# Strassen's seven products in the first layers of the last four blocks of an attention and maxout kernel

## The chip, the cores and the metric

The kernel runs on one core of a Trainium2 chip. The metric is the device time of one execution in microseconds (us), lower is better. TensorE multiplies matrices into PSUM, VectorE and ScalarE carry the results from PSUM to SBUF, GpSimd adds in SBUF and issues the input loads, and SyncE (SP) issues the output stores and the transposing DMAs. Each engine works through its own instructions in program order.

## The reference, cut to what matters

```python
# q, k, v: (8, 8, 576, 64); keys and values are averaged over groups of 8 tokens
k_p = k.reshape(B, H, 72, 8, 64).mean(axis=3)
v_p = v.reshape(B, H, 72, 8, 64).mean(axis=3)
attn = softmax(q @ k_p.T / 8)              # 576 x 72 per batch and head
x = (attn @ v_p), heads side by side       # (4608, 512): 8 batches of 576 tokens
h = max(max(x @ w1, x @ w2), x @ w3)       # (4608, 768)
out = h @ w_out                            # (4608, 512), float32
```

## The kernel before

**The maxout layer.** With w1 taken out, h = x w1 + max(0, x (w2 - w1), x (w3 - w1)). The kernel forms w2 - w1 and w3 - w1 once (`sub_w`, kept in `mw1` and `mw2`), and the product w1 w_out once (`linear`, kept in `wm`). So the first layer is two products followed by a maximum with zero, and the second layer adds two products in one PSUM bank: x times `wm` and the maximum times `mwo`.

**Blocks.** The 4608 tokens are cut into nine blocks of 512 (0 to 8). `block(n, plan)` runs `hidden(n)` and then `project(n)`. In `hidden`, each of six column groups `jc` of 128 takes two parts (`hidden_part`): four matmuls of 512 columns per part into a `pw` bank (line 321); after the first part ScalarE takes the relu into `t` (L327), after the second VectorE takes the larger of `t` and the bank into `hT` (L329). `project` makes four tiles of 128 tokens: four matmuls x by `wm` (L353), six matmuls `hT` by `mwo` (L357) into one `po` bank, a ScalarE copy to `osb` (L362), and two stores on SP.

**Attention in between.** Every part and every half of an output tile is a slot, and `plan(n)` hangs attention steps of batch n + 1 on the slots: `k` (transpose the keys into `kz`, L171 and L176), `s0` to `s7` (scores of one head, 576 columns, and their exponential on ScalarE, L199 and L204), `v0` to `v4` (values of 128 tokens, L234, then a reciprocal and a product on VectorE into `xn`, L240 and L242), `x0` to `x4` (bring `xn` into `xT`; from batch 3 on by a transposing DMA on SP, L219), and `T` (transpose the queries of batch n + 2 into `qT` by a DMA on SP, L265). Since a batch has 576 tokens and a block 512, block 5 (tokens 2560 to 3071) reads batch 4 and the slices x0 and x1 of batch 5, written x50 and x51 below. `pool_work(n)`, at the first slot of block n, puts on GpSimd the loads of batch n + 3 (keys, values, queries; the first waits for the first matmuls of the block) and then the sums over groups of 8 for batch n + 2 (`fold_k`, `fold_v`).

**What sets the order.** There is no scheduler: instructions are issued in the order written, and an engine stops at the first instruction whose inputs or buffer are not ready. PSUM's eight banks are shared out as `tr` 1, `pw` 3, `att` 2 x 2. SP's queue holds query transposes, slices and stores in one line.

Of the kernel before, what the change touches and what calls it, by code (L numbers as in the profile page):

```python
# [14 lines left out]
def kernel(  # L15
# [18 lines left out]
    C = H * D  # L34
# [19 lines left out]
    sb3 = ctx.enter_context(tc.tile_pool(name="sb3", bufs=3))  # L54
    psp = ctx.enter_context(tc.tile_pool(name="psp", bufs=1, space=PSUM))
    ctx.enter_context(tc.manual_schedule())

    kts, vts, qbs, kps, qTs, ets = {}, {}, {}, {}, {}, {}
# [90 lines left out]
    def pool_v(b, h, g, tag, evac):  # L149

        pvp = psp.tile([128, g - h, D], F32, name="pvp", tag=tag[0], bufs=tag[1])
        for j in range(POOL):
            nc.tensor.matmul(pvp, identh[0:Sp, :], vts[b][:, h:g, j, :],  # L153
                             start=(j == 0), stop=(j == POOL - 1))
        evac(out=vp_all[:, b, h:g, 0:D], in_=pvp[0:Sp])

    def turn_q(b, n0, n1, evac, tag):
        if b not in qTs:
            qTs[b] = sb2.tile([128, 2 * NG, 128], BF16, name="qT", tag="qT")
        pqt = psp.tile([128, n1 - n0, 128], BF16, name="pqt", tag=tag[0],  # L160
                       bufs=tag[1])
        qf = qbs[b].rearrange("p hp t d -> p (hp t d)")
        for n in range(n0, n1):
            nc.tensor.transpose(pqt[:, n - n0, :], qf[:, 128 * n:128 * n + 128],  # L164
                                ident)
        evac(out=qTs[b][:, n0:n1, :], in_=pqt)

    def keys(b, tag):
        pkt = psp.tile([128, 6, 96], BF16, name="pkt", tag=tag[0], bufs=tag[1])
        for i in range(6):  # L170
            nc.tensor.transpose(pkt[:, i, :], kps[b][:, i, :, :], ident[0:96, 0:96])  # L171
        return pkt
# [7 lines left out]
    def turn_k(b):  # L180
        pkt = keys(b, ("att", 2))
        for par in range(2):
            fill_kz(b, par, 0, H, pkt, nc.vector.tensor_copy)

    def pool_k(b, tag):

        new_kp(b)
        pkp = psp.tile([128, 6, D], F32, name="pkp", tag=tag[0], bufs=tag[1])
        for j in range(POOL):
            nc.tensor.matmul(pkp, identh[0:96, :], kts[b][:, :, j, :],  # L190
                             start=(j == 0), stop=(j == POOL - 1))
        nc.vector.tensor_copy(out=kps[b][:, :, 0, :], in_=pkp[0:96])
        nc.scalar.copy(out=kps[b][:, :, 1, :], in_=pkp[0:96])
# [15 lines left out]
    def scores(b, h):  # L209
        psc = psp.tile([128, 1024], F32, name="psc", tag="att", bufs=2)  # L210
        score(b, h, psc[:, 0:320], 0, 0, 5)
        score(b, h, psc[:, 320:512], 1, 0, 3)
        score(b, h, psc[:, 512:576], 1, 3, 4)
        exp(ets[b][:, h, :], psc[0:Sp, 0:S])

    def turn_x(b, c0, keep, xn, tag, evac=nc.scalar.copy):
        if b > 2:
            g0 = S * b + c0
            nc.sync.dma_start_transpose(  # L219
                out=xT[:, :, g0 + keep:g0 + 128],  # L220
                in_=xn.rearrange("p g h d -> p (g h d)")[keep:128])
            return
        pxt = psp.tile([128, KCH, 128], F16, name="pxt", tag=tag[0], bufs=tag[1])
        for kc in range(KCH):
            nc.tensor.transpose(  # L225
                pxt[:, kc, :],
                xn[:, kc // 2, 2 * (kc % 2):2 * (kc % 2) + 2, :], identh)
        g0 = S * b + c0
        evac(out=xT[:, :, g0 + keep:g0 + 128], in_=pxt[:, :, keep:128])

    def values(b, c0):
        pav = psp.tile([128, 2, 512], F32, name="pav", tag="att", bufs=2)
        for h in range(H):
            nc.tensor.matmul(  # L234
                pav[:, h // 4, 65 * (h % 4):65 * (h % 4) + 65],
                ets[b][:, h, c0:c0 + 128], vp_all[:, b, h, :],
                start=True, stop=True)
        pv = pav[:, :, 0:260].rearrange("p g (h e) -> p g h e", e=65)
        rcp = sb3.tile([128, 2, 4], F32, name="rcp", tag="rcp")
        nc.vector.reciprocal(out=rcp, in_=pv[:, :, :, 64])  # L240
        xn = sb3.tile([128, 2, 4, D], F16, name="xn", tag="xn", bufs=6)
        nc.vector.tensor_tensor(  # L242
            out=xn, in0=pv[:, :, :, 0:D],
            in1=rcp.to_broadcast([128, 2, 4, D]), op=ALU.mult)
        return xn

    CHUNKS = ((0, 0), (128, 0), (256, 0), (384, 0), (448, 64))
    TR = ("tr", 1)
    PW = ("pw", 3)
# [4 lines left out]
    def do(b, steps):  # L254
# [3 lines left out]
        for name in steps.split():  # L258
# [4 lines left out]
            elif name[0] == "T":  # L263
                qTs[b] = sb2.tile([128, 2 * NG, 128], BF16, name="qT", tag="qT")
                nc.sync.dma_start_transpose(  # L265
                    out=qTs[b], in_=qbs[b].rearrange("p hp t d -> p (hp t d)"))
            elif name[0] == "k":
                turn_k(b)
            elif name[0] == "K":
                fold_k(b, nc.vector)  # L270
            elif name[0] == "p":
                pool_v(b, 4 * i, 4 * i + 4, TR, nc.scalar.copy)
            elif name[0] == "s":
                if i == 0:
                    new_et(b)
                scores(b, i)
            elif name[0] == "d":
                sub_w(i)
            elif name[0] == "w":
                turn_w(i, nc.scalar.copy if i % 2 else nc.vector.tensor_copy)  # L280
            elif name[0] == "v":
                xns[b, i] = values(b, CHUNKS[i][0])
            else:
                turn_x(b, *CHUNKS[i], xns[b, i], ("att", 2),
                       nc.vector.tensor_copy if name[0] == "X" else nc.scalar.copy)
# [11 lines left out]
    def turn_w(jc, evac):  # L297
        pwt = psp.tile([128, KCH, 128], F16, name="pwt", tag=TR[0], bufs=TR[1])
        for kc in range(KCH):
# [3 lines left out]
    def linear():  # L303

        for kc in range(KCH):
            pm = psp.tile([128, C], F32, name="pm", tag="pw", bufs=3)
            for jc in range(JCH):
# [8 lines left out]
    def hidden_part(n, jc, c0, c1, hT):  # L316
        col = slice(NB * n + c0, NB * n + c1)
        for wi in range(1, 3):
            pw = psp.tile([128, c1 - c0], F32, name=f"pw{wi}", tag="pw", bufs=3)
            for kc in range(KCH):  # L320
# [11 lines left out]

    def hidden(n, hT):

        halves = n < 2
        if halves:
# [7 lines left out]

    def project(n, hT):
        for mm in range(4):
# [3 lines left out]
            for c in ((slice(0, C // 2), slice(C // 2, C)) if last else (slice(0, C),)):  # L350
                po = psp.tile([128, c.stop - c.start], F32, name="po", tag="pw", bufs=3)
                for kc in range(KCH):
                    nc.tensor.matmul(po, xT[:, kc, bass.ts(m, 128)], wm_sb[:, kc, c],  # L353
                                     start=(kc == 0), stop=False)
                yield
                for jc in range(JCH):
                    nc.tensor.matmul(po, hT[:, jc, bass.ts(mm, 128)], wo_sb[:, jc, c],  # L357
                                     start=False, stop=(jc == JCH - 1))
# [10 lines left out]

    def new_hT():  # L370
        return sb2.tile([128, JCH, NB], F16, name="hT", tag="hT")


    wm = psp.tile([128, 512], F32, name="wm", tag="tr", bufs=1)

# [4 lines left out]
    new_et(0)  # L380
    ATT = ("att", 2)
    new_kp(0)
    k16 = const.tile([96, 6, 4, D], F16, name="k16", tag="k16")
    pkp0 = psp.tile([128, 6, D], F32, name="pkp", tag="pw", bufs=3)
    heat(10)
# [32 lines left out]
    def scores4(h):  # L418
        psc = psp.tile([128, 4, 256], F32, name="psc4", tag="att", bufs=2)
        for i in range(4):  # L420
# [3 lines left out]
    def scores2(h):  # L424
        psc = psp.tile([128, 2, 512], F32, name="psc2", tag="att", bufs=2)
        for i in range(2):
# [26 lines left out]

    def block(n, plan):

        hT = new_hT()
        slot = 0
        for part in (hidden(n, hT), project(n, hT)):
            for _ in part:
                if slot == 0 and n > 0:  # L460
                    pool_work(n, mms[-1])
                for b, steps in plan.get(slot, ()):
                    if b < B:
                        do(b, steps)
                slot += 1

# [6 lines left out]
              29: [(1, "s4 s5")], 30: [(1, "s6 s7")], 31: [(1, "v0")],  # L473
              32: [(1, "v1 x0")], 33: [(1, "X1 v2")]})
    load_k(3, nc.gpsimd)
# [16 lines left out]
    def plan(n):  # L492
# [5 lines left out]
        return got  # L498

    def pool_work(n, mm):  # L500

        if n + 3 < B:
            after([load_k(n + 3, nc.gpsimd)], mm)
            load_v(n + 3, nc.gpsimd)
            load_q(n + 3)
        if n + 2 < B:
            fold_k(n + 2, nc.gpsimd)
        if n + 2 < B:
            fold_v(n + 2)

    for n in range(1, TOK // NB):
        block(n, plan1() if n == 1 else plan(n))

# [29 lines left out]
```

## Time and profile before

| what | us |
|---|---|
| median of 3 runs (236.77 to 237.47) | 237.34 |
| the profiled execution's own time | 246.42 |
| its span, first to last instruction | 244.6 |
| TensorE busy in the span | 226.3 |
| VectorE, ScalarE, GpSimd busy | 101.6, 107.3, 122.2 |

The own time is the span and some 1.8 us around it. The profile is of one execution. In it, a row of the groups view gives the line, the engine, the operation, what it writes and reads, the shape, the count, the busy time, the mean length of one in ns, and the idle time ahead of it with what ended that. The chain view follows the work that ended last backwards, each step to what released it. Starts of matmuls follow each other more closely than their lengths suggest, since matmuls overlap.

### The profile page before, as it was taken

What the parts mean: (1) busy time and instruction counts of PE and PEld (TensorE: products, weight loads), DVE (VectorE), ACT (ScalarE), POOL (GpSimd) and SP (SyncE); (2) the same over time, 40 slices, a digit from 0 to 9 for tenths busy, and PEclk for the clock granted to TensorE, in tenths of its full rate; (3) what the DMA queues carried; (4) which work ended last, traced back from release to release, by engine and by line L of the source; (5) the groups of instructions that cost most, each with busy time, mean ns of one, the idle gap of its engine ahead of it and who ended that gap; (6) DMA issues with size and microseconds to landing.
All of it is one profiled execution on the core that took longest, in us unless ns stands there. A gap on an engine that the chain in (4) does not pass through costs nothing.

```text
span 244.6 us, 4167 instructions
## 1 busy us (share of the span) xinstructions
PE 226.3 (93%) x1629; PEld 123.9 (51%) x1630; DVE 101.6 (42%) x190; ACT 107.3 (44%) x187; POOL 122.2 (50%) x89
## 2 busy tenths in 40 slices
PE   7688999999999999629999999899999999999993
PEld 2467645568555555204555555355545554444442
DVE  3769664076244436204253526153633452402300
ACT  2355435746845672103722671266137413223311
POOL 8664105999999999108980899993000000000000
PEclk9999999999999999976999999999999999999999
DMA  6999999999698999999996799981452056034024
GB/s 181 203 196 196 216 196 206 186 185 187 131 185 195 133 74 88 155 173 171 162 159 150 117 215 177 153 163 31 89 128 55 3 128 140 3 80 91 0 61 113
DMA packets 47140, 33.51 MB, mean 137 GB/s; under 512 B 27345, under 2 KB 41681, under 8 KB 47121
## 3 DMA queue, kind: packets, MB, share of 16 engines
q0 software_dynamic: 16864, 16.72, 46.8%
q1 hardware_dynamic: 30096, 16.39, 35.8%
q8 instruction: 13, 0.21, 0.4%
q10 hardware_dynamic: 160, 0.13, 0.3%
q14 instruction: 7, 0.05, 0.1%
HBM read 34.60 MB, written 9.44 MB: 180 GB/s over the span
## 4 chain that ended last, share of the span: by engine, by line
PE 83%; DMA 9%; DVE 3%; issue 1%; ACT 1%; POOL 1%; POOLq 0%; DVEq 0%
PE pw L321 38%; PE po L357 17%; PE po L353 12%; DMA xT<-xn 6%; PE psc L199 6%; PE pav L234 4%; DMA vt<-in_v_dram 3%; PE pm L308 2%; PE pxt L225 2%; DVE mw L294 1%; DVE xn L242 1%; PE pkt L171 1%; PE pqt L164 1%; PE pvp L153 1%; POOL qb L87 0%
## 5 line engine op out<-in xcount | busy, mean ns | idle before, releaser
L321 PE MATMUL pw<-xT,mw 128*128 128x512 f16 (+1 forms) x480 | 108.3, 363 | 7.8 <-DMA xT<-xn 7.6
L329 DVE TENSOR_TENSOR hT<-t,pw 128x512 f16<-128x512 f16 (+1 forms) x60 | 37.9, 633 | 69.6 <-PE pw L321 37.4
L321 PEld LDWEIGHTS <-mw 128*128 128x128 f16 x480 | 43.0, 99 | 43.2 <-DMA xT<-xn 7.1
L357 PE MATMUL po<-mwo,hT 128*128 128x512 f16 (+1 forms) x222 | 52.7, 373 | 0.0
L327 ACT ACTIVATE t<-pw 128x512 f16<-128x512 f32 (+1 forms) x60 | 33.3, 554 | 42.2 <-PE pw L321 42.1
L362 ACT COPY osb<-po 128x512 f32<-128x512 f32 (+1 forms) x36 | 20.9, 579 | 61.1 <-PE po L357 61.1
L204 ACT ACTIVATE et<-psc 72x576 f16<-72x576 f32 (+2 forms) x62 | 40.4, 658 | 7.6 <-PE psc L199 7.5
L353 PE MATMUL po<-wm,xT 128*128 128x512 f16 (+1 forms) x148 | 37.1, 373 | 0.0
L131 POOL TENSOR_TENSOR half<-vt 72x2048 f32<-72x2048 f16 x7 | 28.4, 4056 | 14.1 <-DMA vt<-in_v_dram 13.6
L357 PEld LDWEIGHTS <-hT 128*128 128x128 f16 x222 | 20.3, 98 | 19.6
L242 DVE TENSOR_TENSOR xn<-pav,rcp 128x512 f16<-128x512 f32 x40 | 27.7, 691 | 1.6 <-DVE rcp L240 0.2
L132 POOL TENSOR_TENSOR half<-half 72x1024 f32<-72x1024 f32 (+1 forms) x13 | 27.2, 2096 | 1.0
L199 PE MATMUL psc<-qT,kz 128*128 128x64 bf16 (+3 forms) x192 | 25.7, 246 | 0.4 <-DVE kz L176 0.3
L199 PEld LDWEIGHTS <-kz 128*128 128x128 bf16 x192 | 17.8, 98 | 15.6 <-DVE kz L176 1.2
L176 DVE COPY kz<-pkt 64x576 bf16<-64x576 bf16 (+1 forms) x16 | 11.4, 716 | 27.4 <-PE pkt L171 27.2
L234 PEld LDWEIGHTS <-et 72*128 72x128 f16 x320 | 15.5, 98 | 8.8 <-issue 0.5
L353 PEld LDWEIGHTS <-xT 128*128 128x128 f16 x148 | 13.3, 98 | 12.6
L131 POOL TENSOR_TENSOR half<-ktFalse 96x1536 f32<-96x1536 f16 x6 | 18.6, 3104 | 0.1
L234 PE MATMUL pav<-vp,et 72*128 72x65 f16 x320 | 17.1, 194 | 0.6 <-ACT et L204 0.6
L240 DVE RECIPROCAL rcp<-pav 128x8 f32<-128x8 f32 x40 | 8.2, 206 | 20.0 <-PE pav L234 19.8
L72 POOL DMA_DIRECT2D ktFalse<-in_k_dram x7 | 3.9, 557 | 19.9 <-PE pw L321 11.9
L135 POOL TENSOR_TENSOR kp<-half 96x384 bf16<-96x384 f32 x12 | 11.7, 992 | 0.5
(51 smaller groups left out, 118.0 us busy)
## 6 DMA issues: line engine op xcount, KB each, us to landing
out_dram<-osb SPq DMA_DIRECT2D x70, 128.0 KB, 2.4
ktFalse<-in_k_dram POOLq DMA_DIRECT2D x7, 576.0 KB, 7.0
qb<-in_q_dram POOLq DMA_DIRECT2D x7, 576.0 KB, 14.8
vt<-in_v_dram POOLq DMA_DIRECT2D x7, 576.0 KB, 12.6
mw<-in_moe_w_dram POOLq DMA_DIRECT2D x9, 256.0 KB, 10.0
ktTrue<-in_k_dram SPq DMA_DIRECT2D x3, 384.0 KB, 5.0
mwo<-in_moe_w_out_dram POOLq DMA_DIRECT2D x1, 768.0 KB, 13.0
qb<-in_q_dram POOLq DMA_DIRECT2D x2, 288.0 KB, 7.7
```

The source lines that it names most:

```text
L131: e.tensor_tensor(out=f, in0=t[:, :, 0:4, :], in1=t[:, :, 4:8, :], op=ALU.add)
L132: e.tensor_tensor(out=f[:, :, 0:2, :], in0=f[:, :, 0:2, :], in1=f[:, :, 2:4, :], op=ALU.add)
L199: nc.tensor.matmul(out, kz_all[b % 2][:, f % 2, h, :], qTs[b][:, n + i0:n + i1, 64 * (h % 2):64 * (h % 2) + 64], start=True, stop=True)
L204: nc.scalar.activation(out=out, in_=in_, func=FT.Exp, scale=1.0 / 64.0)
L234: nc.tensor.matmul(pav[:, h // 4, 65 * (h % 4):65 * (h % 4) + 65], ets[b][:, h, c0:c0 + 128], vp_all[:, b, h, :], start=True, stop=True)
L242: nc.vector.tensor_tensor(out=xn, in0=pv[:, :, :, 0:D], in1=rcp.to_broadcast([128, 2, 4, D]), op=ALU.mult)
L321: mm = nc.tensor.matmul(pw, w_sb[wi][:, kc, bass.ts(jc, 128)], xT[:, kc, col], start=(kc == 0), stop=(kc == KCH - 1))
L327: nc.scalar.activation(out=t, in_=pw, func=FT.Relu)
L329: nc.vector.tensor_tensor(out=hT[:, jc, c0:c1], in0=t, in1=pw, op=ALU.max)
L353: nc.tensor.matmul(po, xT[:, kc, bass.ts(m, 128)], wm_sb[:, kc, c], start=(kc == 0), stop=False)
L357: nc.tensor.matmul(po, hT[:, jc, bass.ts(mm, 128)], wo_sb[:, jc, c], start=False, stop=(jc == JCH - 1))
L362: nc.scalar.copy(out=osb[:, c], in_=po)
```

## The change

Blocks 0 to 3 keep their form. For blocks 5 to 8 the first layer, a product of a 512 x 768 weight (twice) and a 512 x 512 slab of xT, is computed with seven products of half-size matrices. The contraction is halved (2 of 4 `kc`), the hidden columns are halved (3 of 6 `jc`, named a, b, c), and the tokens are halved (256). `fold_w` forms four sums S1 to S4 of weight quarters, once for each of the two weights, on VectorE in slots of block 4. `fold_x(n)` forms four differences T1 to T4 of the quarters of the block's xT, on VectorE, at the mark `T`. `product(i, g)`, written 1a to 7c, is four matmuls of 256 columns, two `kc` for each of the two weights, which share one bank. Products 1, 6, 5 and 3 add up in one bank A, and ScalarE copies the bank out after each of them; product 2 has a bank B, products 7 and 4 a bank C. VectorE adds the kept copies to banks B and C (`plus`) and takes the maximum with zero over both weights (`best`, a scalar_tensor_tensor) into `hT`.

`ORDER` is one written-out order for all this: products, halves of output tiles of blocks 4 to 7 (`F`, two to a tile), and the attention of batches 5 to 7 (`k6` keys, `s60` a piece of scores, `v52` values with their slice). Scores of batches 6 and 7 are cut into nine pieces of 512 columns (`scores_flat`). PSUM is shared out anew from there on: `pa` 2, `bc` 1, `po` 1, `sc` 2, `val` 2 banks. Block 8's output tiles come last and use `pa`.

Ahead of that, `keys(5)` moves into block 3, and block 4's hidden part carries all scores and two values of batch 5 and the query transpose T of batch 6 (`LEAD`). One half of each key copy goes to ScalarE from batch 3 on. GpSimd's sums move up: keys 5 in block 2, keys 6 in block 3, the rest in block 4, none in block 5. `project` takes the six `jc` in the order 0, 3, 1, 4, 2, 5.

```diff
-    psp = ctx.enter_context(tc.tile_pool(name="psp", bufs=1, space=PSUM))
+    pools = [stage.enter_context(tc.tile_pool(name="psp", bufs=1, space=PSUM))]
...
     def turn_k(b):
-        pkt = keys(b, ("att", 2))
-        for par in range(2):
-            fill_kz(b, par, 0, H, pkt, nc.vector.tensor_copy)
+        pkt = keys(b, ATT if len(pools) == 1 else SC)
+        for par, evac in enumerate((nc.vector.tensor_copy, nc.scalar.copy)):
+            fill_kz(b, par, 0, H, pkt, evac if b > 2 else nc.vector.tensor_copy)
...
+    def scores_flat(b, j):
+        psc = psum([128, 512], F32, name="psf", tag=SC[0], bufs=SC[1])
...
+        exp(ets[b].rearrange("p h s -> p (h s)")[:, 512 * j:512 * j + 512], psc[0:Sp])
...
-                for jc in range(JCH):
+                for jc in (0, 3, 1, 4, 2, 5):
...
+    FOLDS_OF = {1: "k3 v3", 2: "k4 v4 k5", 3: "v5 k6", 4: "v6 k7 v7"}
     def pool_work(n, mm):
         if n + 3 < B:
             after([load_k(n + 3, nc.gpsimd)], mm)
             load_v(n + 3, nc.gpsimd)
             load_q(n + 3)
-        if n + 2 < B:
-            fold_k(n + 2, nc.gpsimd)
-        if n + 2 < B:
-            fold_v(n + 2)
+        for name in FOLDS_OF.get(n, "").split():
+            if name[0] == "k":
+                fold_k(int(name[1]), nc.gpsimd)
+            else:
+                fold_v(int(name[1]))
...
+    PA, BC, PO = ("pa", 2), ("bc", 1), (("po", 1), ("pa", 2))
+    FIRST = {1: (0, 0), 2: (1, 2), 7: ("S3", "T3")}
+    PRODUCTS = FIRST | {3: ("S4", 3), 4: (3, "T4"), 5: ("S1", "T1"), 6: ("S2", "T2")}
...
+    LEAD = {0: [(5, "s0")], 1: [(5, "s1"), (6, "T")], 2: [(5, "s2")], 3: [(5, "s3")],
+            4: [(5, "s4")], 5: [(5, "s5")], 6: [(5, "s6")], 7: [(5, "s7")],
+            8: [(5, "v0 x0")], 9: [(5, "v1 x1")]}
...
+    def fold_x(n):
+        x, t = halves(n), pad[:, 0:4]
+        minus(t[:, 0], x[1], x[0])
+        minus(t[:, 1], x[3], t[:, 0])
+        minus(t[:, 2], x[3], x[1])
+        minus(t[:, 3], x[2], t[:, 1])
...
+        def kept(i, g):
+            return pad2[:, 0] if i == 1 else pad[:, 2 * (i - 3) + (3 * n + g) % 2]
...
+        def plus(out, i, g, p):
+            nc.vector.tensor_tensor(out=out, in0=kept(i, g), in1=p, op=ALU.add)
+        def best(row, c):
+            nc.vector.scalar_tensor_tensor(
+                out=hTs[n][:, row, :].rearrange("p (a c) -> p a c", a=2), in0=c[:, :, 0, :],
+                scalar=0.0, in1=c[:, :, 1, :], op0=ALU.max, op1=ALU.max)
+        def product(i, g):
...
+            of = "B" if i == 2 else "C" if i in (4, 7) else "A"
+            if i in FIRST:
+                tag = {"A": PA, "B": SC, "C": BC}[of]
+                banks[of, g] = psum([128, 2, HALF], F32, name=f"p{of}", tag=tag[0],
+                                    bufs=tag[1])
+            p = banks[of, g]
+            for w in range(2):
+                a, b = sw[w + 1][PRODUCTS[i][0]], x[PRODUCTS[i][1]]
+                for kc in range(2):
+                    mm = nc.tensor.matmul(p[:, w], a[:, kc, bass.ts(g, 128)], b[:, kc, :],
+                                          start=(i in FIRST and w + kc == 0),
+                                          stop=(w + kc == 2), skip_group_check=True)
...
+            if i in (1, 6, 5):
+                nc.scalar.copy(out=kept(i, g), in_=p)
+            if i == 2:
+                plus(top(g)[:, 0], 1, g, p)
+            elif i == 3:
+                nc.scalar.copy(out=top(g)[:, 1], in_=p)
+                best(g, top(g))
+            elif i == 4:
+                plus(low[:, 0], 6, g, p)
+                best(g + JH, low)
+            elif i in (5, 7) and (12 - i, g) in done:
+                plus(low[:, 1], 5, g, banks["C", g])
...
+    ORDER = """
+        F 1a 2a T 1b F k6 2b 6a 6b F 5a 7a s60 s61 v52 3a 5b s62 4a s63 F v53 s64 1c
+        7b s65 F v54 s66 6c 4b s67 s68 F 2c 7c v60 5c 3b F 3c F k7 4c 1a F s70 2a 1b
+        T v61 s71 F 2b 6a s72 F 5a 6b v62 7a 3a s73 F 4a s74 v63 5b s75 7b s76 F 1c
+        v64 s77 s78 4b 6c F v70 5c 7c 2c 3b F 4c 3c F v71 T 1a 2a F 1b F 2b 6a 6b
+        v72 F 5a 7a F v73 5b 4a 3a F 7b v74 1c F 6c 4b 2c F 5c 7c 3b F 4c 1a T 3c 2a
+        F 1b 2b 6a 7a 6b 5a F 3a 5b 4a F 1c F 7b 3b 6c F 4b 5c F 7c 2c 3c F 4c F
+    """
...
-    for n in range(1, TOK // NB):
-        block(n, plan1() if n == 1 else plan(n))
+    folds = [f for wi in range(1, 3) for f in [fold_w(wi)] * 4]
+    block(1, plan1(), (hidden, project))
+    for n in range(2, 4):
+        block(n, with_keys(n) if n == 4 - 1 else plan(n),
+              (hidden, project))
+    block(4, LEAD, (hidden,), folds)
...
+    weave()
+    for _ in project(TOK // NB - 1):
+        pass
```

## The prediction

> **What bounds the kernel now.** I read the busy shares first, then the chain that ended last, then that chain in order of time. Times below are us from the span's start; "+n" is us after block 4's first matmul.
>
> ```profile
> PE 226.3 (93%) x1629; PEld 123.9 (51%) x1630; DVE 101.6 (42%) x190; ACT 107.3 (44%) x187; POOL 122.2 (50%) x89
> ...
> PE 83%; DMA 9%; DVE 3%; issue 1%; ACT 1%; POOL 1%; POOLq 0%; DVEq 0%
> ```
>
> TensorE carries 83% of the chain, and DMA is the only other large share. The chain in time shows where each sits:
>
> ```profile
> 98.64 9.93 DMA xT<-xn
> 108.66 1.86 PE pw L321 x4
> ...
> 152.57 4.57 DMA xT<-xn
> 157.39 1.02 PE pw L321 x4
> ...
> 202.63 10.36 PE pw L321 x48
> ...
> 239.99 0.67 PE po L357 x6
> ```
>
> From 157.39 to the end TensorE never waits: 48 first-layer matmuls take 10.36 (0.216 each), a block with attention 22.53, one without 19.0. Before that it waited twice for a transposed slice of xT. At 102.0 it stood 6.64 and then ran slowly: block 3 took 25.06 instead of 22.53. That is 9.17 together; the profiled execution (span 244.6, own time 246.42) is 9.08 above the median 237.34, so I take the median as this execution without that stop. Before block 5 it lost 1.14 (block 4 took 23.67 instead of 22.53). The timeline shows why:
>
> ```profile
> 135.05 0.56 POOL L72 DMA_DIRECT2D ktFalse<-in_k_dram  x1 [7.09 <-PE pkt L171]
> ...
> 138.77 9.43 SPq L265 DMA_TRANSPOSE qT<-qb  x1
> ...
> 148.74 2.46 SPq L219 DMA_TRANSPOSE xT<-xn  x1
> ...
> 152.57 2.74 SPq L219 DMA_TRANSPOSE xT<-xn  x2
> ```
>
> ```profile
> DMA to landing us min/median/max: 14.6/14.6/14.6
> ```
>
> Block 4 begins at 133.72. GpSimd issues batch 7's three loads at +1.3 to +3.9; SP issues batch 6's query transpose (T6) at +5.05 and is held 9.4 by it. The last line is T6's own: it lands 14.6 after issue, +19.7. The slice x50, behind it on SP's queue, lands at +20.3 (5.3 after issue), x51 at +23.4. In block 3 the same pair behaves alike: T5 lands 16.5 after 111.37, +19.2. Without loads beside it a query transpose lands in 4.0 (issue 61.5) or 4.4 (161.9). So the DMA work at a block's start is full for some 19 us.
>
> Durations that I use come from the groups by shape:
>
> ```profile
> L321 PE MATMUL pw<-xT,mw 128*128 128x256 f16 x96 | 13.3, 272 | 0.3 <-DVE xT L229 0.3
> L329 DVE TENSOR_TENSOR hT<-t,pw 128x512 f16<-128x512 f16 x48 | 33.0, 688 | 66.8 <-PE pw L321 36.1 <-ACT et L204 30.6
> L294 DVE TENSOR_TENSOR mw<-mw,mw 128x1024 f16<-128x1024 f16 x6 | 3.9, 683 | 0.0
> L362 ACT COPY osb<-po 128x512 f32<-128x512 f32 x35 | 20.5, 585 | 60.6 <-PE po L357 60.6
> ```
>
> [...] matmul busy time misleads, since matmuls overlap. The trace agrees: a 512-column one reads 386 ns but follows its predecessor after 216, so I use the chain's lengths. [...] 1024 columns in 683 ns, 512 from PSUM in 688. [...] after 6.64 idle, four matmuls took 1.86, after 0.95 idle 1.02.
>
> **The change, part by part.**
>
> *TensorE work.* Each of blocks 5 to 8 loses 48 matmuls of 512 columns (10.36) and gains 7 x 3 x 4 = 84 of 256. In block 0 eight of these take 0.87, the last output tile's six 0.66: 0.11 each, so 9.22. A weight load (99 ns) still fits under one. Saved 1.14 a block, **4.55** in all. Scores of batches 6 and 7 become nine 512-column pieces for eight of 576: the same columns, zero. One product (4 matmuls) takes 0.44.
>
> *VectorE and ScalarE.* A block loses 6 maxima (0.69) and 6 relus (0.60). VectorE gains 4 subtractions for T1 to T4 (0.42: from 683 for 1024 and 553 for 768 columns, 0.51 ns a column and 0.16 fixed), 9 sums out of PSUM (0.69) and 6 "best" operations; ScalarE gains 12 PSUM copies (0.585). A best is not in the trace: [...] I take 0.69[...]. With five values (0.90 each) and a key copy (0.755) VectorE then has 17.2 in a block of 21.4, ScalarE about 15. Neither is full; their order matters.
>
> *Hand-overs.* A wait for a copy costs 0.2 (end of matmuls to start of copy, in the timeline) + 0.585 + 0.05 = 0.84; for a sum 0.94. Following the issue order item by item with these lengths, I find room everywhere (tightest: product 4a to 7b in block 6, 1.2 against 0.94) but for two places. In block 8, T1 to T4 stand on VectorE ahead of the sum for 2a, which reads the only buffer of product 1; ScalarE's copy of 1b waits for it, and 6b for the copy: ready 5.55 after the end of 4c, due at 3.94. **Cost 1.6, and 0.15 at 5a behind.** In block 7 the same order costs 0.1. The other is the start of block 5.
>
> *Start of block 5.* Block 4 now carries scores from slot 0 and two values: 12 x 0.865 + 8 x 0.25 + 2 x 0.26 = 12.9. Then half an output tile 0.865, 1a and 2a (ends +14.65), T1 to T4 go to VectorE, 1b, 1.295, keys 6, 2b; product 6a is due at +17.1 and needs T2. T1 needs x50 and x51 in xT. Their values are ready sooner (x50 at +11.2 for +14.9 before), but both slices stand on SP behind T6, whose place, with batch 7's loads beside it, is unchanged. Taking T6 at +19.7 and 0.6 for each slice (as x50 took), x51 lands at +20.9. T2 is ready at 21.8: 6a waits 4.7. Queued on VectorE behind T1: T2 to T4 (22.6), then its key copy (23.4). ScalarE's new half of the key copy waits for that (24.0), and its copy of 6a stands behind (24.6), so 5a, otherwise at 23.55, loses 1.1 more. **Cost 5.8**, in place of the 1.14 of before.
>
> *The rest, at nothing.* The eight weight sums (0.55) lie in VectorE's gaps of block 4 (10.1 busy of 23.7 before). GpSimd's sum of keys 5 (6.9) moves ahead of batch 6's loads, which start some 3 later in block 3; T5 gets a head start. Bounds: 1 lost at block 4's start if T5 lands later, 1 won. Keys on ScalarE, the half-tile order of jc, and the single "po" bank (at least 1.3 between tiles against 0.84) are covered by matmuls.
>
> Sum: -4.55 - 1.14 + 5.8 + 1.75 + 0.1 = **+1.96**: this execution with its stop at 248.4, the median at **239.3**. [...] at 102 that took 2.5. I leave it to the range.
>
> **Rivals.**
> - *The slices land in time.* With x51 by +16 only 0.7 is lost at 5a: -4.55 - 1.14 + 0.7 + 1.85 = -3.1, **234.2**. For it: 4.0 to 4.4 for a lone query transpose. Against it: 14.6 and 16.5 beside loads. The point that decides is x51 at +19; each us later costs one.
> - *VectorE becomes the bound*[...] Against it: nothing in the trace[...].
> - *The products don't save*: if weight loads set the pace, 84 would cost what 48 did, 239.3 + 4.55 = 243.9. Against it: the 96 matmuls of that shape.
>
> **Numbers.** About 0.3% (0.7 us) is what a measurement tells here. Late slices: 0.50 (own range 237.9 to 242). In time: 0.27. VectorE bound or no saving: 0.14. Part of the delay, cancelling the gain: 0.09. So faster 0.27, same 0.09, slower 0.64; range 233.6 to 243.5.
>
> **What would show it.** In the changed profile: first-layer products at 0.44 per four; a TensorE wait of 4 to 5 at block 5's first 6a, with T1 on VectorE waiting for DMA xT<-xn; a wait of about 1.6 at block 8's first 6b; best near 0.69. I am wrong if the first wait is under 2, or if the products run slower than 0.12 each.

## The result: 3.7% slower, beyond the range, because VectorE's weight sums waited for GpSimd

The changed kernel takes 246.44 us (median of 4 runs, 245.18 to 252.22) against 237.41 for the kernel before in the same session (4 runs, 236.77 to 237.69). The ratio is **1.0367, 95% interval 1.032 to 1.0414**. The profiled execution took 246.26, its span 244.5. Some executions of a kernel ran with a lower granted TensorE clock and some per cent longer (two of e9's 23 at 0.985 and 244.8, the others at 0.996 to 1.000 and at most 237.73): ratios leave those out, medians don't, so the two can differ, and the profiles of before, e6, e7 and e9 are of such executions.

The page of the changed kernel, busy shares and the engines' shares of the chain that ended last:

```profile
PE 223.9 (92%) x1771; PEld 139.2 (57%) x1772; DVE 144.1 (59%) x245; ACT 122.5 (50%) x218; POOL 123.8 (51%) x89
...
PE 78%; DVE 13%; issue 5%; ACT 3%; DVEq 0%; ACTq 0%
```

VectorE went from 101.6 to 144.1 busy and from 3% to 13% of the chain. The added work alone does not come to these 42.5 us: e1 below runs the same instructions on VectorE and has it busy for 129.7. So 28.1 is added work, and 14.4 is something else. TensorE's timeline (start, length, instruction, idle time before it and what ended it) shows where it stood:

```profile
137.15 1.86 PE L342 MATMUL pw<-xT,mw 128*128 128x512 f16 x4 [2.82 <-DVE hT L350]
...
142.04 1.89 PE L342 MATMUL pw<-xT,mw 128*128 128x512 f16 x8 [0.90 <-DVE hT L350]
...
150.82 1.01 PE L618 MATMUL pA<-xT,mw 128*128 128x256 f16 x4 [4.79 <-DVE hT L350]
...
154.85 1.04 PE L618 MATMUL pA<-pad,sw 128*128 128x256 f16 x8
...
217.29 1.09 PE L618 MATMUL pA<-pad,sw 128*128 128x256 f16 x8 [0.95 <-ACT pad L624]
```

Block 4 starts at 125.28. All of the long waits are for a maximum into hT (L350) in block 4's hidden part; the one at 150.82 is product 1b, whose bank still held a hidden part that VectorE had not read. The forecast looked for its wait one step later, at 6a (154.85), and for a DMA; there is no wait at 6a. The windows view adds the granted clock (columns: stretch, length, busy time of PE, PEld, DVE, ACT, POOL, granted clock, DMA share, GB/s):

```profile
125.28:143.77 18.49, 14.77 (x90) 7.50 (x88) 14.64 (x11) 8.88 (x15) 18.09 (x11) 0.91 1.00 160
143.77:157.35 13.58, 8.03 (x46) 4.49 (x45) 12.73 (x15) 3.07 (x6) 9.90 (x5) 0.87 0.23 50
```

The hidden part was to take 12.9 and took 18.5. Of the 5.6 more, 3.7 are waits, and most of the rest is matmuls that ran slowly after them: the four of 512 columns behind the wait of 2.82 took 1.86 where others take 1.03. In the second stretch it is the same: after the wait of 4.79 the four matmuls of product 1b took 1.01 where four of that shape take 0.60. The granted clock is 0.91 and 0.87 in the two stretches, where block 4 before had 1.00. After a wait of 2.13 in e8 the matmuls kept their pace: eight of 256 columns took 0.89 up to the next start, 0.11 each. Slow matmuls after a wait the forecast had left to its range.

The cause stands on VectorE's timeline, the weight sums (L551, L560) and the first of T1 to T4:

```profile
130.35 3.53 DVE L560 TENSOR_TENSOR sw<-mw 128x768 f16<-128x768 f16 x1
133.80 2.69 DVE L551 TENSOR_TENSOR sw<-mw 128x768 f16<-128x768 f16 x1
136.42 0.68 DVE L350 TENSOR_TENSOR hT<-t,pw 128x512 f16<-128x512 f16 x1
137.02 1.02 DVE L551 TENSOR_TENSOR sw<-sw,mw 128x768 f16<-128x768 f16 x1
138.07 3.33 DVE L551 TENSOR_TENSOR sw<-mw,sw 128x768 f16<-128x768 f16 x1
...
141.91 1.56 DVE L560 TENSOR_TENSOR sw<-mw 128x768 f16<-128x768 f16 x1
...
144.23 0.55 DVE L551 TENSOR_TENSOR sw<-mw 128x768 f16<-128x768 f16 x1
...
146.14 4.03 DVE L551 TENSOR_TENSOR sw<-sw,mw 128x768 f16<-128x768 f16 x1
150.09 0.68 DVE L350 TENSOR_TENSOR hT<-t,pw 128x512 f16<-128x512 f16 x1
150.69 2.10 DVE L551 TENSOR_TENSOR sw<-mw,sw 128x768 f16<-128x768 f16 x1
...
153.31 0.89 DVE L551 TENSOR_TENSOR pad<-xT 128x512 f16<-128x512 f16 x1
```

The same instruction takes 0.55 or 4.03. The eight together take 18.8 instead of 4.4, while the maxima between them, whose second input is in PSUM, keep their 0.68. Beside it GpSimd's timeline:

```profile
129.36 4.09 POOL L136 TENSOR_TENSOR half<-vt 72x2048 f32<-72x2048 f16 x1
133.53 2.55 POOL L137 TENSOR_TENSOR half<-half 72x1024 f32<-72x1024 f32 x1
136.15 1.47 POOL L140 TENSOR_TENSOR vp<-half 72x512 f16<-72x512 f32 x1
137.70 3.28 POOL L136 TENSOR_TENSOR half<-ktFalse 96x1536 f32<-96x1536 f16 x1
...
145.71 4.04 POOL L136 TENSOR_TENSOR half<-vt 72x2048 f32<-72x2048 f16 x1
149.83 2.54 POOL L137 TENSOR_TENSOR half<-half 72x1024 f32<-72x1024 f32 x1
152.44 1.46 POOL L140 TENSOR_TENSOR vp<-half 72x512 f16<-72x512 f32 x1
```

Add starts and lengths and lay the two lists side by side: GpSimd's instructions end at 133.45, 136.08, 137.62, 140.98 and 149.75, and VectorE's sums end at 133.88, 136.49, 138.04, 141.40 and 150.17, each 0.41 to 0.43 later. These sums met a running GpSimd sum and stood until it was over. The standing time is the 14.4 (18.8 less 4.4). The maxima that run beside the same GpSimd sums, with one input in SBUF and one in PSUM, do not stand: 0.68, 0.67 and 0.68 at 136.42, 141.32 and 150.09. What makes a sum stand is not shown here, only that it does and for how long. The kernel before had no such meeting: in its block 4 VectorE ran maxima, values and copies, all of which read PSUM.

### The profile page after: what moved, and what is told of

Same layout as the page of the kernel before. It is cut to its first block, busy times and chain, and to the rows that moved or that the text cites. A ratio compares the mean times of both kernels' runs of the same rounds, so it can differ in the third digit from the quotient of the medians.

```text
span 244.5 us, 4527 instructions
## 1 busy us (share of the span) xinstructions
PE 223.9 (92%) x1771; PEld 139.2 (57%) x1772; DVE 144.1 (59%) x245; ACT 122.5 (50%) x218; POOL 123.8 (51%) x89
## 4 chain that ended last, share of the span: by engine, by line
PE 78%; DVE 13%; issue 5%; ACT 3%; DVEq 0%; ACTq 0%
PE po L386 19%; PE pw L342 17%; PE po L382 11%; PE pA L618 7%; PE pC L618 4%; PE psc L204 4%; PE pav L253 4%; DVE sw L551 3%; PE wm L404 2%; PE pm L329 2%; PE pxt L243 2%; PE psf L204 2%; PE pB L618 1%; DVE pad L551 1%; DVE sw L560 1%
## 5 line engine op out<-in xcount | busy, mean ns | idle before, releaser
L342 PE MATMUL pw<-xT,mw 128*128 128x512 f16 (+1 forms) x288 | 62.5, 349 | 4.0 <-DVE hT L350 3.7
L386 PE MATMUL po<-mwo,hT 128*128 128x512 f16 (+1 forms) x222 | 53.9, 380 | 0.0
L350 DVE TENSOR_TENSOR hT<-t,pw 128x512 f16<-128x512 f16 (+1 forms) x36 | 21.4, 596 | 30.6 <-ACT et L209 19.8
L342 PEld LDWEIGHTS <-mw 128*128 128x128 f16 x288 | 25.4, 99 | 19.8 <-issue 5.4
L209 ACT ACTIVATE et<-psc 72x576 f16<-72x576 f32 (+2 forms) x46 | 30.1, 664 | 5.8 <-PE psc L204 5.6
L624 ACT CAST pad<-pA 128x512 f16<-128x512 f32 x36 | 20.6, 586 | 24.6 <-DVE pad L596 13.0
L348 ACT ACTIVATE t<-pw 128x512 f16<-128x512 f32 (+1 forms) x36 | 18.9, 526 | 18.8 <-PE pw L342 18.8
L596 DVE TENSOR_TENSOR pad<-pad,pC 128x512 f16<-128x512 f16 x24 | 16.4, 685 | 9.9 <-PE pC L618 5.1
L618 PEld LDWEIGHTS <-sw 128*128 128x128 f16 x192 | 18.3, 98 | 6.1 <-issue 2.0
L204 PE MATMUL psc<-qT,kz 128*128 128x320 bf16 (+2 forms) x144 | 19.1, 246 | 0.4 <-DVE kz L181 0.3
L618 PEld LDWEIGHTS <-mw 128*128 128x128 f16 x144 | 13.9, 98 | 9.8 <-issue 5.3
L259 DVE RECIPROCAL rcp<-pav 128x8 f32<-128x8 f32 x40 | 8.2, 204 | 18.5 <-PE pav L253 18.4
L136 POOL TENSOR_TENSOR half<-ktFalse 96x1536 f32<-96x1536 f16 x6 | 18.8, 3130 | 0.3
```

The lines of the kernel that those rows point to most:

```text
L136: e.tensor_tensor(out=f, in0=t[:, :, 0:4, :], in1=t[:, :, 4:8, :], op=ALU.add)
L204: nc.tensor.matmul(out, kz_all[b % 2][:, f % 2, h, :], qTs[b][:, n + i0:n + i1, 64 * (h % 2):64 * (h % 2) + 64], start=True, stop=True)
L209: nc.scalar.activation(out=out, in_=in_, func=FT.Exp, scale=1.0 / 64.0)
L342: mm = nc.tensor.matmul(pw, w_sb[wi][:, kc, bass.ts(jc, 128)], xT[:, kc, col], start=(kc == 0), stop=(kc == KCH - 1))
L350: nc.vector.tensor_tensor(out=hT[:, jc, c0:c1], in0=t, in1=pw, op=ALU.max)
L618: mm = nc.tensor.matmul(p[:, w], a[:, kc, bass.ts(g, 128)], b[:, kc, :], start=(i in FIRST and w + kc == 0), stop=(w + kc == 2), skip_grou ...
```

## The experiments

**Theory C (collision):** the weight sums, and T1 to T4 behind them, stand while GpSimd runs its own sums, and hold up the maxima. **Rivals:** the late slices of the forecast alone; or sums that are slow on their own; or simply more work on VectorE; or a cost of the place in the order.

**e1: no late sums on GpSimd.** In block 4 GpSimd writes constants for values 6, keys 7 and values 7.

```diff
-            if name[0] == "k":
+            if name == "k7":
+                new_kp(b)
+                nc.gpsimd.memset(kps[b], 0.5)
+            elif name in ("v6", "v7"):
+                nc.gpsimd.memset(vp_all[:, b, :, 0:D], 0.5)
+            elif name[0] == "k":
```

> The changed kernel, but in block 4 GpSimd writes a constant into the summed keys of batch 7 and the summed values of batches 6 and 7 instead of adding them up (that part of the computation is left out); everything on VectorE, TensorE, ScalarE and SP is as in the changed kernel. Theory C (VectorE's weight sums, two SBUF inputs each, stand still while a GpSimd instruction that reads SBUF runs): the eight sums take 0.55 each, block 4's hidden part takes 12.9 instead of 18.5, and what is left is the late slices that the prediction put at 5.8 with its 1.6 in block 8: 239 (238 to 241). Theory S (collisions, and the slices then land in time): 234 to 235. Theory O (the sums are slow for a reason of their own, such as weights read by TensorE at the same time): sums still 1 to 4 each, 246.

Measured: 241.74 (239.68 to 244.58, 4 runs), ratio 1.0225 [1.0151, 1.0298]. From e1's timelines of VectorE and TensorE, and the landing of query transposes (last line, minimum, median, maximum):

```profile
129.67 0.55 DVE L566 TENSOR_TENSOR sw<-mw 128x768 f16<-128x768 f16 x1
...
146.59 0.42 DVE L557 TENSOR_TENSOR pad<-xT 128x512 f16<-128x512 f16 x1 [6.32 <-DMA out_dram<-osb]
```

```profile
147.53 1.89 PE L624 MATMUL pA<-pad,sw 128*128 128x256 f16 x8 [5.74 <-DVE pad L557]
```

```profile
DMA to landing us min/median/max: 3.9/4.0/14.6
```

All eight sums take 0.55 and block 4's hidden part 12.9, so the sums are not slow on their own. The first of them runs beside GpSimd's last write of a constant (129.59 to 130.14) and is not held by it. So the collision with GpSimd's sums is shown, and under it lies what the forecast had priced: T6 lands 14.6 after its issue, T1 stands until 146.59 (the releaser named is a store just behind x51 on SP), and 6a waits 5.74. From block 4's first matmul to the end of the last one e1's profiled execution (239.68, the fastest of the four) takes 109.33; the forecast's sum gives 106.94 + 1.96 = 108.9. The median lies above the range that was expected (238 to 241); where the other executions lost the rest was not traced.

**e2: the sums alone, in the kernel before.**

```diff
+    def fold_w(wi):
+...
+        for k, x, y in ((0, a[2], a[3]), (2, a[0], a[2]), (1, s[:, 0], a[0]), (3, a[1], s[:, 1])):
+            nc.vector.tensor_tensor(out=s[:, k], in0=x, in1=y, op=ALU.subtract)
+            yield
+    FOLDS = (3, 4, 5, 6, 7, 8, 9, 11)
+...
+                if n == 4 and slot in FOLDS:
+                    next(folds.pop(0))
```

> The kernel before plus nothing but eight VectorE operations of the weight sums' shape (128x768, two SBUF inputs) in the same slots of block 4, whose results nobody reads. Theory C: GpSimd adds keys and values from about +4 to the end of that block, so each operation is held to the end of a GpSimd instruction, as in the changed kernel; VectorE ends its eighth 8 to 10 late, the maximum for the last column groups is late with it, and the time is 245 to 248. Theory O (slow on their own) gives the same here. If they cost only their busy time (8 x 0.55 = 4.4 in gaps): 237.4 to 238.

Measured: 245.58 (244.94 to 246.04), ratio 1.0345 [1.0309, 1.0381]. VectorE's timeline of e2, then TensorE's waits (total, times, longest):

```profile
137.32 6.42 DVE L460 TENSOR_TENSOR sw<-mw 128x768 f16<-128x768 f16 x2
143.66 0.67 DVE L329 TENSOR_TENSOR hT<-t,pw 128x512 f16<-128x512 f16 x1
```

```profile
PE po L353 <- DVE hT L329: 5.1, 1, 5.1
PE pw L321 <- DVE hT L329: 1.5, 2, 1.3
```

Eight instructions of 0.55 cost the kernel before some 8 us, with no Strassen product in it. They need not be part of the change to do their harm.

**e3: as many, with one input in PSUM.** Each instruction reads 512 columns of a weight and a PSUM bank, which two extra matmuls fill.

```diff
+            nc.vector.tensor_tensor(out=s[:, k].rearrange("p a c -> p (a c)")[:, 0:512],
+                                    in0=w_sb[wi][:, k, 0:512], in1=ps, op=ALU.subtract)
```

> The kernel before plus eight VectorE operations in the same slots, 128x512, with one input in SBUF (a weight) and the other in PSUM, and two matmuls of 512 columns that fill that bank; results nobody reads. They are longer in busy time (0.69 each, 5.5 in all) than the weight sums. Theory C: with a single SBUF input none is held, each takes 0.69, and the time is 237.5 to 238.5. If any added VectorE work in these slots costs the time (theory Q, VectorE's order alone): 241 or more. Theory O, in the form that weights read by VectorE collide with TensorE's reads: slow here too, 245.

Measured: 236.94 (236.62 to 239.34, 12 runs), ratio 0.9991 [0.9964, 1.0017]. The group of the eight in e3:

```profile
L460 DVE TENSOR_TENSOR sw<-mw,pz 128x512 f16<-128x512 f16 x8 | 5.2, 680 | 0.0
```

They hold VectorE for more time than 8 x 0.55 and stand in the same slots beside the same GpSimd sums, and cost nothing. So neither more work on VectorE nor the place is the cause. What e3 takes away is the second SBUF input, and with it the pace of the sums: 680 ns for 512 columns against 0.55 for 768. No run has two SBUF inputs at the slower pace beside a GpSimd sum, so the two are not separated.

**e4: the sums early.** The changed kernel with the weight sums in block 0.

```diff
-    FOLDS = (3, 4, 5, 6, 7, 8, 9, 11)
+    FOLDS = (14, 15, 16, 18, 19, 20, 21, 22)
...
-    block(4, LEAD, (hidden,), folds)
+    block(4, LEAD, (hidden,))
```

> The changed kernel with its eight weight sums moved to block 0 (slots 14 to 22), when GpSimd waits for a load and reads nothing; T1 to T4 and GpSimd's sums stay where they were. Theory C: the sums cost nothing (0.55 each), block 4 takes 12.9, but T1 to T4 of block 5, two SBUF inputs as well, now come while GpSimd still adds (until about +28 after block 4's start), so each of the four is held to the end of a GpSimd instruction on top of the late slices: 241 to 245. Without collisions at T1 to T4: 239. If the sums were not the cause: 246.

Measured: 247.58 (245.25 to 249.49), ratio 1.0342 [1.0293, 1.0392], no better, and above the 241 to 245 that was expected. VectorE's timeline of e4, T1 to T3:

```profile
148.47 1.20 DVE L485 TENSOR_TENSOR big<-xT 128x512 f16<-128x512 f16 x1 [6.30 <-DMA xT<-xn]
149.70 2.44 DVE L485 TENSOR_TENSOR big<-xT,big 128x512 f16<-128x512 f16 x1
152.07 1.48 DVE L485 TENSOR_TENSOR big<-xT 128x512 f16<-128x512 f16 x1
```

The maxima do not wait any more, but now T1 waits for its slice first, and then T1 to T3 stand behind GpSimd's sum of values 7 (until 153.27 by its own timeline). Product 6a, which needs T2, loses 8.5 in one wait; in e1, with the late slices alone, it lost 5.74.

**e10 and e5: the place of T6.** T6 goes behind x50 and x51 on SP: e10 with nothing else changed, e5 on top of e1.

```diff
-    LEAD = {0: [(5, "s0")], 1: [(5, "s1"), (6, "T")], ...
+    LEAD = {0: [(5, "s0")], 1: [(5, "s1")], ...
...
-            8: [(5, "v0 x0")], 9: [(5, "v1 x1")]}
+            8: [(5, "v0 x0")], 9: [(5, "v1 x1"), (6, "T")]}
```

> As e1 (GpSimd writes constants in place of the sums of values 6, keys 7 and values 7, which are left out), and the query transpose T6 stands on SP behind the slices x50 and x51 instead of ahead of them. If the slices are late because they stand behind T6 on SP's queue, they land as soon as their values are written, product 6a's and the value product's wait of 5.7 us at block 5 goes with the slow matmuls behind it, and the time is e1's 241.7 less about 6: 235.5 (234 to 237.5), faster than before; T6, which then starts later, may hold the first scores of batch 6 for a microsecond. If the slices were late because batch 7's loads fill the DMA engines whatever the order on SP, block 5's wait stays at 4 to 6 and the time at 240 to 243.

> The whole computation: the changed kernel with T6 behind x50 and x51 on SP, and nothing else. It fills the fourth corner beside the changed kernel (246.4), e1 (no late sums on GpSimd, T6 ahead: 241.7) and e5 (neither: 236.4). Theory: the held sums on VectorE alone set the start of block 5 in the changed kernel, T1 comes behind the last of them, later than x51 lands; so T6's place is hidden and moving it gives next to nothing: 246 (244 to 247.5), with the waits for hT of 3 to 5 us still there. Rival: both delays add up whatever the order, 246.4 less 5.3: 241 (239.5 to 242.5).

| ratio to before | T6 ahead of the slices | T6 behind them |
|---|---|---|
| GpSimd sums in block 4 | 1.0367 [1.032, 1.0414] (the change) | 1.0333 [1.0263, 1.0402] (e10) |
| constants in their place | 1.0225 [1.0151, 1.0298] (e1) | 0.9954 [0.9932, 0.9977] (e5) |

Medians: e10 245.48 (245.37 to 245.85), e5 236.39 (234.62 to 242.09, 20 runs). SP's queue in e5, and TensorE at 6a:

```profile
136.50 3.11 SPq L237 DMA_TRANSPOSE xT<-xn  x2
139.72 3.15 SPq L286 DMA_TRANSPOSE qT<-qb  x1
```

```profile
143.91 1.05 PE L624 MATMUL pA<-pad,sw 128*128 128x256 f16 x8 [1.40 <-DVE pad L557]
```

TensorE's waits in e10:

```profile
PE pA L618 <- DVE hT L350: 4.8, 1, 4.8
PE pw L342 <- DVE hT L350: 3.7, 2, 2.6
```

Moved alone, T6 gives almost nothing, because T1 stands behind the held sums until after the slice is there. The changed kernel's own queue shows it: the values for the slices stand behind held sums too, so the two slices go out only from 144.34 on, when T6 no longer holds the queue (130.55 + 9.78), and land 2.4 after their issue, well before T1 at 153.31:

```profile
144.34 3.10 SPq L237 DMA_TRANSPOSE xT<-xn  x2
```

With the collision gone, T6's place gives some 5 to 6 (241.74 less 236.39 by the medians, 6.4 by the ratios). The two delays do not add up, the longer hides the shorter. That is why the forecast's own wait did not show in the changed profile.

**e6 and e7: two mends that failed.** Both have the sums of e4 and keys 6 ahead of T in block 5, and put values 6 ahead of batch 7's loads on GpSimd. In e6 GpSimd still sums keys 7 and values 7; in e7 VectorE does, in blocks 5 and 6.

```diff
     def pool_work(n, mm):
+        if n == 4:
+            fold_v(6)
         if n + 3 < B:
             after([load_k(n + 3, nc.gpsimd)], mm)
```

> The whole computation. Changed kernel with: the eight weight sums in block 0, where GpSimd is idle; in block 4 GpSimd sums values 6 ahead of batch 7's loads, so that T6 goes out without loads beside it, and then keys 7 and values 7; keys 6 is issued ahead of T in block 5, and 2a ahead of T in block 8. Theory (an add or subtraction on VectorE with two SBUF operands stands while GpSimd runs such a one): hT is in time in block 4, x51 lands in time, but T1 to T4 of block 5 still fall beside GpSimd's sums of keys 7 or values 7, and take 1 to 3 us each: 238 (235 to 241), with one TensorE wait of 3 to 5 us at block 5's first copy or product. If the sums were slow for their own place in the order and not for GpSimd, T1 to T4 take 0.42 each and the time is about 233.5.

> The whole computation. As e6, but keys 7 and values 7 are summed on VectorE in blocks 5 and 6 (six steps), so that GpSimd is idle from about 10 us into block 4 on. Theory: T1 to T4 take 0.42 to 0.5, no TensorE wait over 1 us is left in blocks 4 to 8, and of the 4.55 saved in the products and the 1.14 of block 5 the most arrives: 233 (231.5 to 235.5), faster than before (237.5) by 1 to 2.5%. Rival (VectorE is the bound in blocks 5 and 6 once it has the extra sums, some 4 us): waits for bank C or the hidden, 235.5 to 239, no faster than before by more than 1%.

Measured: e6 247.59 (245.77 to 251.74), ratio 1.0409 [1.0355, 1.0463]; e7 248.54 (243.87 to 249.04, no ratio: three of the four lie at 248.4 or above). Both forecasts were wrong. SP's queue in e6, then GpSimd's and VectorE's timelines of e7:

```profile
131.54 6.13 SPq L286 DMA_TRANSPOSE qT<-qb  x1
138.21 10.99 SPq L237 DMA_TRANSPOSE xT<-xn  x2
```

```profile
39.19 4.04 POOL L136 TENSOR_TENSOR half<-vt 72x2048 f32<-72x2048 f16 x1 [13.38 <-DMA vt<-in_v_dram]
```

```profile
39.31 4.33 DVE L485 TENSOR_TENSOR sw<-mw,sw 128x768 f16<-128x768 f16 x1
```

With values 6 first the loads went out at 131.90 in e6, not ahead of T6's start but just behind it, and the slices came into the middle of them: 10.99 on SP for the two, and 17.2 of waiting at block 5 (8.1 in e7). That execution of e6 took 251.74, the other three 245.77 to 247.61, so the 17.2 is likely more than the kernel loses there in those. T1 to T3 in e6 stood as in e4 (1.86, 2.44, 1.48). In e7 they took 0.42, as expected, but in block 0 the last weight sum met GpSimd's first sum, 0.12 after its start, and TensorE waited 4.4 for the copy behind it. So e7 as run does not show what the extra sums on VectorE cost.

**e8: both causes away, e9: T6's place alone in the kernel before.** e8 is e7 with the loads first again, values 6 behind them, T6 as in e5, and the weight sums two to a slot.

```diff
-    FOLDS = (14, 15, 16, 18, 19, 20, 21, 22)
+    FOLDS = (14, 14, 15, 15, 16, 16, 18, 18)
```

> The whole computation. Both causes taken away: as e7 (weight sums in block 0, two to a slot and so over before GpSimd's first sum; keys 7 and values 7 summed on VectorE in blocks 5 and 6; keys 6 ahead of T in block 5, 2a ahead of T in block 8), but batch 7's loads go first in block 4, values 6 is summed behind them and ends some 12 us into the block, and T6 stands on SP behind x50 and x51. If GpSimd's sums and T6's place are all that cost time: T1 to T4 at 0.42 each, a wait at block 5 of at most 1.5, none of over 1 later: 235.5 (234 to 237), faster than before by 0.3 to 1.4%, and not above e5, which leaves the same sums out. If the six steps on VectorE hold back bank C or the hidden: 237 to 240.

> The kernel before with T6 behind x51 in block 4, nothing else. It tells what e5 and e8 owe to T6's place and what to the products. Block 5's wait of 1.14 in the profile of before goes: 236.3 (235.8 to 237). If batch 6's scores in block 5 then wait for T6, 237.4 or more.

Measured: e8 236.56 over all 9 runs (233.9 to 244.91) against 237.11, its ratio **0.9928 [0.9891, 0.9964]**; e9 236.54 (235.77 to 244.84, 23 runs), ratio 0.9973 [0.9959, 0.9987]. GpSimd's last sum and TensorE at 6a in e8:

```profile
135.98 1.27 POOL L140 TENSOR_TENSOR vp<-half 72x512 f16<-72x512 f32 x1
```

```profile
144.85 0.39 PE L626 MATMUL pA<-big 128*128 128x256 f16 x2 [2.13 <-DVE big L485]
```

GpSimd is idle from 137.25 on, T1 to T4 take 0.42 each, and no wait but this one is left in blocks 4 to 8: the six sums on VectorE are covered. The wait of 2.13 is longer than the 1.5 that was expected at most. By its ratio e8 is the fastest whole kernel here. From block 4's first matmul to the end of the last one it takes 103.39 for 106.94 before, and -4.55 - 1.14 + 2.13 gives -3.56 for that -3.55. Of this its profiled execution (234.67) gives back 0.9 ahead of block 4 (start at 125.53, where before stood at 133.72 less its stop of 9.08). e9 owes its 0.3% to block 5's wait of before: its profile has none there, where before's had 0.95. The intervals of e8 and e9 lie side by side and barely overlap, so the products' part over e9 is small and at the edge of what these runs tell: some 0.45%, the quotient of the two ratios, near what the profile gives (-4.55 + 2.13 + 0.9 = -1.5, 0.64%). Three of the 4.55 saved are spent again on the wait for x51 and ahead of block 4.

## Why the prediction was wrong, point by point

- **The step that failed** is *The rest, at nothing*: "The eight weight sums (0.55) lie in VectorE's gaps of block 4 (10.1 busy of 23.7 before)". The gaps were VectorE's own. The windows view of block 4 before (columns as above) has GpSimd, the fifth engine figure, busy for 21.4 of the same 23.7, and the question how long a sum on VectorE takes beside one on GpSimd was not asked:

```profile
133.72:157.39 23.67, 22.72 (x160) 11.73 (x159) 10.13 (x18) 11.22 (x19) 21.43 (x12) 1.00 1.08 166
```

  So a term that was put at nothing cost the most: at 18.8 for 4.4 the sums, with the waits and slow matmuls behind them, moved 6a from a free +17.1 to +29.57, 12.5 us; the forecast had it at +21.8 for another reason.
- **From one time to the other.** The forecast's sum for block 4 to the end was +1.96; measured is 115.22 - 106.94 = +8.3. With 12.5 and 0.56 at 5a for the 5.8, and 0.95 for block 8's and block 7's 1.85, the sum is -4.55 - 1.14 + 12.5 + 0.56 + 0.95 = +8.3. The rest from 237.34 up to 246.26 is 0.64 ahead of block 4, within the bound of 1 given for the moved keys.
- **Start of block 5** was right in kind, and nearly in size, where it could be seen: in e1 T6 lands after 14.6, 6a starts at +22.9 for +21.8 and waits 5.74 for 4.7, and the 1.1 at 5a does not come. In the changed kernel it lay hidden under the collision, with no wait at 6a.
- **TensorE work** was right: the group of the changed kernel below has the 256-column matmuls at 272 ns, and their starts in the timeline give 0.44 for four; e8's sum needs the whole 4.55.
- **VectorE became the bound** was a rival, but for the wrong reason: its price rested on a slow best, an assumption of the author's that no trace showed. Measured, a best takes 691 ns for 512 columns, the value taken (0.69) and near the 685 of a sum from bank C (L596):

```profile
L599 DVE SCALAR_TENSOR_TENSOR hT<-pad 128x512 f16<-128x512 f16 x24 | 16.4, 691 | 2.7 <-ACT pad L628 2.1
...
L618 PE MATMUL pA<-xT,sw 128*128 128x256 f16 x48 | 7.2, 272 | 0.0
```

- **Block 8's 6b** waited 0.95, not 1.6: right in place, too long by 0.65. With 2a ahead of T (e6 to e8) the wait is gone.
- **The sign** (slower, 0.64) was right, but in the changed kernel by luck: the late slices on which it rested cost nothing there, and the loss of 9 (246.44 less 237.41) came from the sums. That the late slices alone would have made it slower too is what e1 shows (1.0225).

## What to carry to other kernels

Before an operation is costed at nothing because its engine has gaps, look at what the other engines do in those gaps: in these runs an add or subtraction of two SBUF tiles on VectorE, 0.55 when free, stood as long as the GpSimd sum that it met and took up to 4.33, and all that was queued behind it stood with it. What helped was one input in PSUM (e3, 680 ns each) or a time at which GpSimd was idle (e8, 0.55 to 0.56 each). When two delays end at the same instruction, take both away before judging either: each mend alone looked useless here (e4, e10).

## What the runs showed of the hardware that I had not expected

- A weight sum of 0.55 on VectorE ended 0.41 to 0.43 after the GpSimd instruction that held it, however long that was: it took 1.02 to 4.03, and in block 0 of e7 4.33. T1 to T3 in e4, 0.42 when free, ended 0.28 to 0.29 after theirs. Both tails are 0.13 short of the free length, so by these lengths, an estimate, all but 0.13 of the instruction runs after the other one's end.
- GpSimd pays too, but little: with a sum waiting, its next instruction takes 0.2 longer (2.55 for 2.34 in e8, 1.47 for 1.27). The sum at 144.23 kept its 0.55 although it falls into GpSimd's pair of key sums (143.13 to 145.63). That pair took 2.50 where the pair at 108.20 took 1.95, 0.55 more, so here GpSimd may have stood for the sum; the view doesn't resolve where the first of the pair ends, and it stays open.
- With loads issued 2.3 after block 4's start and T6 behind the slices, the two slices held SP's queue for 3.11 (e5); with T6 in front and the loads just behind its start, at +5.7, for 10.99 (e6, the execution of 251.74). The two kernels differ in both respects, and which counts more was not separated.
